# One unit of exponentials per segment on GpSimd: a transformer block on one core

## The chip, the cores and the metric

The kernel runs on one core of a Trainium2 chip. Its engines are TensorE (PE in the profile, with its weight loads as PEld), VectorE (DVE), ScalarE (ACT), GpSimd (POOL) and SyncE (SP), which issues the DMAs. The metric is the device time of one execution in microseconds. A measurement of this kernel is told apart from no change at 2%.

## What is computed

A pre-norm block on 2048 tokens of width 640: an attention of 32 heads of width 20, then a GLU of inner width 1728 without an activation function. Inputs are bf16, of small random values.

```python
def _A_ref(x, wqkv, wo):                       # H = 32, Dh = 20
    q, k, v = split_heads(x @ wqkv)
    p = softmax(einsum("bhqd,bhkd->bhqk", q, k) * Dh ** -0.5)
    return merge_heads(einsum("bhqk,bhkd->bhqd", p, v)) @ wo

def _B_ref(x, w_gate, w_up, w_down):
    return ((x @ w_gate) * (x @ w_up)) @ w_down

h  = x + _A_ref(_layernorm(x), wqkv, wo)
h2 = h + _B_ref(_layernorm(h), w_gate, w_up, w_down)
```

The softmax needs 32 x 2048 x 2048 exponentials, 134 million. That is the work that the change touches.

## The kernel before

**Units, tiles, segments.** The queries are cut into 4 blocks of 512 (`b`), the heads into 8 groups of 4 (`g`), the keys into 16 tiles of 128 (`kt`). A *unit* is the score block of one head, one key tile and one query block: 128 keys on the partitions by 512 queries. All 2048 units stand in one list, in the order b, g, kt, head in the group (`j`). A *segment* is one (b, g), so 64 units; there are 32. The list is cut into *tiles* of three units, without regard to where segments begin, which makes 683 tiles.

**One round of the loop.** For each tile, `emit_S` allocates a score tile `sc` of three PSUM banks (there are two such tiles), lets PE compute three score blocks (L285, K = 32 rows each, in separate row groups of the array), and lets ACT take the exponential of all 1536 columns at once, into a bf16 tile `E` in SBUF (L292; six buffers). There is no maximum subtracted; the scale is in the activation. The three units then wait in the queue `av_q`. Next, `go_on` lets a job that has begun run on for up to 640 ns of estimated PE work. `emit_AV` takes at most four units of tiles at least two rounds old and multiplies each with V, and a column of ones for the sums, into the accumulator `acc` (L330, one PSUM bank, the four heads on separate column groups). At a segment's end DVE copies `acc` to `asb` (L337), and `norm` sends the sums through DRAM and back, so that they lie on all partitions; five rounds later DVE takes their reciprocal (L305), and eight rounds after that it multiplies (L313) `asb` by the spread reciprocals into `On`.

**Jobs.** Everything else on PE comes as jobs in between: the transposes and projections of the first part, and for each finished query block the output projection with the residual and the second layer norm (`job_out`), the GLU (`job_glu`) and the down projection (`job_y`). They share one PSUM bank `mi`, which DVE empties (L167, L464, L509, L525), so a next job's matmuls wait until DVE has done that. The last query block's jobs run after the loop, on the banks of `sc`, and ACT empties the GLU's first product there (`u`, L507).

**Order.** The program's order is the order of emission: each engine runs its own instructions in that order and waits on semaphores for other engines. S of tile i+2 needs the PSUM of tile i, so it waits for tile i's exponential. GpSimd only fills constants before the loop: the identity and the ones of V (L113 to L115).

Of the kernel before, what the change touches and what calls it, by code (L numbers as in the profile page):

```python
# [9 lines left out]
BF16 = mybir.dt.bfloat16  # L10
F32 = mybir.dt.float32
I32 = mybir.dt.int32
ACT = mybir.ActivationFunctionType
ALU = mybir.AluOpType

P = 128
# [4 lines left out]
NT = S // P  # L21
# [7 lines left out]
QB = 512  # L29
NB = S // QB  # L30
TPB = QB // P
UPT = 3
# [3 lines left out]
SM_SCALE = float(DH) ** -0.5  # L36
# [8 lines left out]
def kernel(  # L45
# [11 lines left out]
    nc = tc.nc  # L57
# [5 lines left out]
    pool = lambda name, bufs=1, **kw: ctx.enter_context(tc.tile_pool(name=name, bufs=bufs, **kw))  # L63
    dram = pool("dram", 2, space=bass.MemoryType.DRAM)
    const = pool("const")
# [3 lines left out]
    ep = pool("ep", 6)  # L69
    nrm = pool("nrm", 2)  # L70
    small = pool("small", 2)
    scp = pool("scp", 2, space=bass.MemoryType.PSUM)
    accp = pool("accp", 1, space=bass.MemoryType.PSUM)
    mip = pool("mip", 1, space=bass.MemoryType.PSUM)
# [3 lines left out]
    rx = tc.alloc_tile_pool(name="rx", bufs=2, side="right")  # L78

    ident = const.tile([P, P], BF16, name="ident")  # L80
    make_identity(nc, ident[:])
    wo = [const.tile([P, D], BF16, name=f"wo{g}") for g in range(NG)]

# [79 lines left out]
    def evac(eng, dst, src):  # L163
        if eng == "act":
            nc.scalar.copy(dst, src)  # L165
        else:
            nc.vector.tensor_copy(dst, src)  # L167
# [3 lines left out]
    def bank(dt=F32, w=512):  # L171
        if not end["on"]:
            return mip.tile([P, w], dt, name="mi", tag="mi")

        if end["k"] == UPT:
            end["t"], end["k"] = scp.tile([P, UPT * 512], F32, name="sc"), 0
        k = end["k"]
        end["k"] += 1
        ps = end["t"][:, k * 512:(k + 1) * 512]
        return ps if dt == F32 else ps.bitcast(dt)[:, 0:w]  # L180
# [33 lines left out]
    units = [(b, g, kt, j) for b in range(NB) for g in range(NG) for kt in range(NT) for j in range(HPG)]  # L214
    tiles = [units[i:i + UPT] for i in range(0, len(units), UPT)]
    av_q = deque()
    acc = {"key": None, "t": None, "from": 0}
    done = set()
    jobs = deque()
# [21 lines left out]
    def step():  # L241

        if cur["gen"] is None:
            if not jobs:
                return None
            cur["key"], cur["gen"] = jobs.popleft()
        try:
            c = next(cur["gen"])
        except StopIteration:
            done.add(cur["key"])  # L250
            cur["gen"], c = None, END
        cur["fresh"] = c in (END, NEXT)
        return c

    def ensure(key):
        while key not in done:
            if step() is None:
                raise RuntimeError(f"no job for {key}")
# [20 lines left out]
    def emit_S(i):  # L279
        sc = scp.tile([P, UPT * 512], F32, name="sc")  # L280
        for b, g, kt, j in tiles[i]:
            ensure(("k", g, kt // TPB))
            ensure(("q", b, g))
        for k, (b, g, kt, j) in enumerate(tiles[i]):
            nc.tensor.matmul(  # L285
                sc[:, k * 512:k * 512 + QB],
                lhsT=kT[g][SLOT * j:SLOT * (j + 1), kt * P:(kt + 1) * P],
                rhs=qT[g][SLOT * j:SLOT * (j + 1), b * QB:(b + 1) * QB],
                start=True, stop=True)
        n = len(tiles[i]) * 512  # L290
        e = ep.tile([P, UPT * 512], BF16, name="E")
        nc.scalar.activation(e[:, 0:n], sc[:, 0:n], ACT.Exp, scale=SM_SCALE)  # L292
        for k, u in enumerate(tiles[i]):
            av_q.append((i, u, e[:, k * 512:k * 512 + QB]))

    def norm(b, g, asb):

        r16 = nrm.tile([P, 16], F32, name="r16")
        sums = dram.tile([HPG, QB], F32, name="sums")
        nc.sync.dma_start(sums[:], asb[DH:P:SLOT, :])  # L300
        nc.sync.dma_start(r16[:], sums[:].rearrange("j (c f) -> (j c) f", f=16))

        def back():
            ri = nrm.tile([P, 16], F32, name="ri")
            nc.vector.reciprocal(ri[:], r16[:])  # L305
            scr = dram.tile([HPG, QB], F32, name="scr")
            nc.sync.dma_start(scr[:].rearrange("j (c f) -> (j c) f", f=16), ri[:])
            bc = nrm.tile([P, QB], F32, name="bc")
            for j in range(HPG):
                nc.sync.dma_start(bc[SLOT * j:SLOT * (j + 1), :], scr[j:j + 1, :].to_broadcast([SLOT, QB]))  # L310

            def mult():
                nc.vector.tensor_tensor(On[b % 2][g][:], asb[:], bc[:], ALU.mult)  # L313
                done.add(("n", b, g))
            later(8, mult)
        later(5, back)

    def emit_AV(upto, most):
        n = 0
        while av_q and av_q[0][0] <= upto and n < most:  # L320
            i, (b, g, kt, j), e = av_q[0]
            if acc["key"] != (b, g):
                if now["i"] < acc["from"]:
                    break
                acc["key"] = (b, g)
                acc["t"] = accp.tile([P, QB], F32, name="acc")
            ensure(("v", kt, g // (NG // 2)))
            av_q.popleft()
            h = HPG * g + j
            nc.tensor.matmul(  # L330
                acc["t"][SLOT * j:SLOT * (j + 1), :],
                lhsT=vx[kt][:, VS * h:VS * h + SLOT], rhs=e,
                start=(kt == 0), stop=(kt == NT - 1))
            n += 1
            if kt == NT - 1 and j == HPG - 1:
                asb = nrm.tile([P, QB], F32, name="asb")
                nc.vector.tensor_copy(asb[:], acc["t"][:])  # L337
                norm(b, g, asb)
                acc["key"] = None
                acc["from"] = now["i"] + 2  # L340
                break
        return n
# [139 lines left out]
    def load_w(fp, st):  # L482
        w = min(FPW, FF - fp * FPW)
        st["w", fp] = []
        for nm, src in (("wu", B_w_up), ("wg", B_w_gate)):
            wt = late["w"].tile([P, KT, FPW], BF16, name=nm)
            nc.sync.dma_start(wt[:, :, 0:w], src[:, fp * FPW:fp * FPW + w].rearrange("(c p) f -> p c f", p=P))
            st["w", fp].append(wt)

    def job_glu(b, st):  # L490
        hp, sp = late["h"], late["s"]
        st["hh"] = [hp.tile([P, QB], BF16, name=f"hh{f}") for f in range(2 * FP)]
        for fp in range(FP):
            w = min(FPW, FF - fp * FPW)
            if fp + 1 < FP:
                load_w(fp + 1, st)
            for f2 in range(2):
                M = min(P, w - f2 * P)
                for k in range(2):
                    ps = bank()  # L500
                    for c in range(KT):
                        nc.tensor.matmul(ps[0:M, :], lhsT=st["w", fp][k][:, c, f2 * P:f2 * P + M], rhs=st["ln2T"][:, c, :],  # L502
                                         start=(c == 0), stop=(c == KT - 1))
                        if c == KT - 1:
                            if k == 0:
                                u = sp.tile([P, QB], F32, name="u")
                                evac("act" if end["on"] else "dve", u[0:M, :], ps[0:M, :])  # L507
                            else:
                                nc.vector.tensor_tensor(st["hh"][2 * fp + f2][0:M, :], ps[0:M, :], u[0:M, :], ALU.mult)  # L509
                        yield 216  # L510
                    yield NEXT
# [19 lines left out]
    def add_tail(b):  # L531
        st = {}
        if b == 0:
            do(("open",), open_late)
        do(("load", b), lambda: (load_tail(b, st), load_w(0, st)))
        add(("out", b), job_out(b, st))
        add(("glu", b), job_glu(b, st))
        add(("y", b), job_y(b, st))
# [5 lines left out]
    i = 0  # L544
    while i < n_tiles or av_q:
        now["i"] = i
        if i < n_tiles:
            emit_S(i)
        used = go_on(BUDGET)
        emit_AV(i - 2, 4)  # L550
        run_events(i)
        if b_seen < NB and ("n", b_seen, NG - 1) in done:
            add_tail(b_seen)
            b_seen += 1
        if not used:
            begin(START)
        i += 1
# [39 lines left out]
```

## Time and profile before

| what | value |
|---|---|
| device time, two runs | 1119.3 and 1120.42 us, median 1119.86 |
| span of the profiled execution | 1124.7 us (no other time of it is given) |
| mean granted TensorE clock in it | 0.814 of full speed |
| L285 scores on PE | 2048 matmuls, mean 460 ns, 323.3 us |
| L330 multiplication with V on PE | 2048 matmuls, mean 470 ns, 311.3 us |
| L337 copy of `acc` on DVE | 32, mean 688 ns |
| L313 normalising product on DVE | 32, mean 685 ns |
| L509 GLU product on DVE | 42, mean 691 ns |

The records of PE overlap: matmuls of different row or column groups run beside each other, and their ends are modelled, so counts times means exceed the busy time. The records of ACT overlap too, since one exponential starts before the former is written out. A wait is put down to the engine that released it. In a slice line each digit is a fortieth of the span, in tenths; the clock line is what the throttle granted to TensorE.

### The profile page before, as it was taken

To read this page: it belongs to the slowest core of one execution; us is meant where nothing else is said; L and a number is where in the kernel's file an instruction comes from. 1 tells how busy PE (TensorE), PEld (TensorE's weight loads), DVE (VectorE), ACT (ScalarE), POOL (GpSimd) and SP (SyncE) were. 2 spreads that over 40 slices of the span, in tenths; PEclk is the share of its full clock that TensorE was granted. 3 is DMA by queue.
4 is the path that set the end of the run, shared out by engine and by line. 5 is a ranking of instruction groups with operands and counts; after the bars stand their busy time and mean duration, and the time that the engine had idled before them with its cause. 6 is when DMAs were issued, how large, how long until landed. Compare 5 with 4: busy or idle time off the path is not lost.

```text
span 1124.7 us, 14910 instructions
## 1 busy us (share of the span) xinstructions
PE 978.5 (87%) x6000; PEld 322.7 (29%) x6000; DVE 296.2 (26%) x690; ACT 953.1 (85%) x726; POOL 3.4 (0%) x54
## 2 busy tenths in 40 slices
PE   3768999999889999978899999888999998884667
PEld 1222332222223223322232234222332233222224
DVE  6452333322005332100034321100253321003211
ACT  4456999999999999999999999999999999990010
POOL 1000000000000000000000000000000000000000
PEclk9668999999558999955588999755779998556699
DMA  4000000100041220100111210000112200003120
GB/s 158 24 1 1 11 11 11 31 20 11 11 136 35 57 71 16 35 11 11 58 34 33 60 51 24 22 11 26 33 34 63 71 17 28 11 11 81 45 66 24
DMA packets 63493, 41.19 MB, mean 37 GB/s; under 512 B 18688, under 2 KB 58560, under 8 KB 63424
## 3 DMA queue, kind: packets, MB, share of 16 engines
q1 hardware_dynamic: 63424, 40.24, 12.7%
q8 instruction: 47, 0.77, 0.3%
q14 instruction: 22, 0.18, 0.1%
HBM read 37.08 MB, written 3.15 MB: 36 GB/s over the span
## 4 chain that ended last, share of the span: by engine, by line
PE 48%; ACT 36%; issue 8%; DVE 5%; DMA 1%; SPq 1%; DVEq 0%; ACTq 0%
ACT E L292 35%; PE sc L285 10%; PE acc L330 9%; PE mi L502 6%; PE mi L195 5%; PE mi L522 5%; PE sc L502 3%; PE mi L461 3%; PE sc L522 2%; PE mi L205 1%; PE mi L185 1%; DVE st L121 1%; ACT lnT L165 1%; PE sc L461 1%; DVE hh L509 1%
## 5 line engine op out<-in xcount | busy, mean ns | idle before, releaser
L292 ACT ACTIVATE E<-sc 128x1536 bf16<-128x1536 f32 (+1 forms) x683 | 925.5, 1692 | 47.5 <-PE sc L285 45.8
L285 PE MATMUL sc<-qT,kT 32*128 32x512 bf16 x2048 | 323.3, 460 | 63.7 <-ACT E L292 59.1
L330 PE MATMUL acc<-E,vx 128*32 128x512 bf16 x2048 | 311.3, 470 | 0.5 <-ACT E L292 0.5
L285 PEld LDWEIGHTS <-kT 32*128 32x128 bf16 x2048 | 99.3, 94 | 297.8 <-issue 293.0
L330 PEld LDWEIGHTS <-vx 128*32 128x32 bf16 x2048 | 67.3, 96 | 224.5 <-issue 221.2
L195 PE MATMUL mi<-lnT,wp 128*128 128x512 bf16 x310 | 91.6, 398 | 5.3 <-DVE qT L167 2.7
L165 ACT COPY u<-sc 128x512 f32<-128x512 f32 (+1 forms) x14 | 8.2, 585 | 80.9 <-PE sc L502 80.9
L337 DVE COPY asb<-acc 128x512 f32<-128x512 f32 x32 | 22.0, 688 | 167.7 <-PE acc L330 167.6
L502 PE MATMUL mi<-ln2T,wu 128*128 128x512 bf16 (+1 forms) x210 | 62.0, 394 | 0.4
L522 PE MATMUL mi<-wd,hh 128*128 128x320 bf16 x336 | 60.6, 302 | 0.0
L502 PE MATMUL mi<-ln2T,wg 128*128 128x512 bf16 (+1 forms) x210 | 60.0, 383 | 0.1
L167 DVE COPY u<-mi 128x512 f32<-128x512 f32 (+1 forms) x42 | 29.0, 691 | 79.1 <-PE mi L502 79.1
L509 DVE TENSOR_TENSOR hh<-mi,u 128x512 bf16<-128x512 f32 (+1 forms) x42 | 29.0, 691 | 77.1 <-PE mi L502 77.1
L522 PEld LDWEIGHTS <-hh 128*128 128x128 bf16 x448 | 37.5, 97 | 39.6 <-issue 28.8
L205 PE MATMUL mi<-wv,lnT 128*128 128x320 bf16 x160 | 34.8, 360 | 8.8 <-DVE vx L167 8.7
L167 DVE CAST kT<-mi 128x512 bf16<-128x512 f32 x31 | 21.4, 691 | 65.7 <-PE mi L195 65.7
L461 PE MATMUL mi<-wo,on 128*128 128x320 bf16 x192 | 37.6, 323 | 0.0
L195 PEld LDWEIGHTS <-wp 128*128 128x128 bf16 x320 | 23.2, 100 | 46.4 <-issue 38.7
L313 DVE TENSOR_TENSOR on<-asb,bc 128x512 bf16<-128x512 f32 x32 | 21.9, 685 | 55.2 <-DMA bc<-scr 55.2
L167 DVE CAST qT<-mi 128x512 bf16<-128x512 f32 x31 | 21.3, 687 | 53.7 <-PE mi L195 53.7
L502 PEld LDWEIGHTS <-wu 128*128 128x128 bf16 (+1 forms) x280 | 21.7, 101 | 45.8 <-issue 35.2
L502 PEld LDWEIGHTS <-wg 128*128 128x128 bf16 (+1 forms) x280 | 21.4, 100 | 42.4 <-issue 31.8
(58 smaller groups left out, 338.8 us busy)
## 6 DMA issues: line engine op xcount, KB each, us to landing
bc<-scr SPq DMA_DIRECT2D x128, 64.0 KB
wu<-in_B_w_up_dram SPq DMA_DIRECT2D x24, 320.0 KB
wg<-in_B_w_gate_dram SPq DMA_DIRECT2D x24, 320.0 KB
xs<-in_A_x_dram SPq DMA_DIRECT2D x4, 640.0 KB
xr<-in_A_x_dram SPq DMA_DIRECT2D x16, 160.0 KB
out_dram<-xr SPq DMA_DIRECT2D x16, 160.0 KB
wd<-in_B_w_down_dram SPq DMA_DIRECT2D x13, 160.0 KB
E<-in_A_wqkv_dram SPq DMA_DIRECT2D x5, 320.0 KB
```

Source lines behind the costliest of these rows:

```text
L167: nc.vector.tensor_copy(dst, src)
L195: nc.tensor.matmul(ps[:], lhsT=wpad[m][c][:].rearrange("p h e -> p (h e)")[:, g * P:(g + 1) * P], rhs=lnT[:, c, ch * QB:(ch + 1) * QB], st ...
L205: nc.tensor.matmul(ps[:, 0:HALF], lhsT=lnT[:, c, t * P:(t + 1) * P], rhs=wv[c][:, half * HALF:(half + 1) * HALF], start=(c == 0), stop=(c ...
L285: nc.tensor.matmul(sc[:, k * 512:k * 512 + QB], lhsT=kT[g][SLOT * j:SLOT * (j + 1), kt * P:(kt + 1) * P], rhs=qT[g][SLOT * j:SLOT * (j + 1 ...
L292: nc.scalar.activation(e[:, 0:n], sc[:, 0:n], ACT.Exp, scale=SM_SCALE)
L313: nc.vector.tensor_tensor(On[b % 2][g][:], asb[:], bc[:], ALU.mult)
L330: nc.tensor.matmul(acc["t"][SLOT * j:SLOT * (j + 1), :], lhsT=vx[kt][:, VS * h:VS * h + SLOT], rhs=e, start=(kt == 0), stop=(kt == NT - 1))
L337: nc.vector.tensor_copy(asb[:], acc["t"][:])
L461: nc.tensor.matmul(ps[:, 0:HALF], lhsT=On[b % 2][g][:, t * P:(t + 1) * P], rhs=wo[g][:, cs], start=(g == 0), stop=(g == NG - 1))
L502: nc.tensor.matmul(ps[0:M, :], lhsT=st["w", fp][k][:, c, f2 * P:f2 * P + M], rhs=st["ln2T"][:, c, :], start=(c == 0), stop=(c == KT - 1))
L509: nc.vector.tensor_tensor(st["hh"][2 * fp + f2][0:M, :], ps[0:M, :], u[0:M, :], ALU.mult)
L522: nc.tensor.matmul(ps[:, 0:HALF], lhsT=st["hh"][f][0:K, t * P:(t + 1) * P], rhs=late["Wd"][f][0:K, cs], start=(f == 0), stop=(f == 2 * FP ...
```

## The change

In tiles that hold three units of key tile 1 of a segment, the third unit's columns are left out of ACT's exponential. DVE copies them from PSUM to SBUF as fp32, scaled (`xp`); GpSimd raises e to them, elementwise, into a bf16 tile `apart`. Because tiles do not begin with segments, such a tile exists in the segments whose number leaves 1 or 2 when divided by 3, which are 21 of 32. The unit is held back from `av_q` and put in front of it when the first unit of the segment's last key tile comes up. Both new tiles have one buffer. The GLU's `u` becomes bf16 with one buffer, where it had fp32 and two.

```diff
+    powp = pool("powp", 1)
...
+    base_e = const.tile([P, 1], F32, name="base_e")
+    nc.gpsimd.memset(base_e[:], 2.718281828459045)
...
+    held = {}
...
         n = len(tiles[i]) * 512
         e = ep.tile([P, UPT * 512], BF16, name="E")
+        apart = None
+        if len(tiles[i]) == UPT and tiles[i][2][2] == 1 and tiles[i][0][2] == 1:
+            n -= 512
+            xp = powp.tile([P, 512], F32, name="xp")
+            nc.vector.tensor_scalar(xp[:], sc[:, n:n + 512], SM_SCALE, None, ALU.mult)
+            apart = powp.tile([P, 512], BF16, name="apart")
+            nc.gpsimd.tensor_tensor(apart[:], base_e[:].to_broadcast([P, 512]), xp[:], ALU.pow)
         nc.scalar.activation(e[:, 0:n], sc[:, 0:n], ACT.Exp, scale=SM_SCALE)
         for k, u in enumerate(tiles[i]):
-            av_q.append((i, u, e[:, k * 512:k * 512 + QB]))
+            if apart is not None and k == 2:
+                held[u[0:2]] = (i, u, apart[:])
+            else:
+                av_q.append((i, u, e[:, k * 512:k * 512 + QB]))
...
                 acc["t"] = accp.tile([P, QB], F32, name="acc")
+            if kt == NT - 1 and (b, g) in held:
+                av_q.appendleft(held.pop((b, g)))
+                continue
             ensure(("v", kt, g // (NG // 2)))
...
                             if k == 0:
-                                u = sp.tile([P, QB], F32, name="u")
+                                u = sp.tile([P, QB], BF16, name="u", bufs=1)
                                 evac("act" if end["on"] else "dve", u[0:M, :], ps[0:M, :])
```

## The prediction

> **What bounds the kernel now.** I read the busy shares and the slices of the page first, then the list of waits, then the exponential's row and its timeline, and last the timeline around the tiles that the change touches.
>
> ```profile
> PE 978.5 (87%) x6000; PEld 322.7 (29%) x6000; DVE 296.2 (26%) x690; ACT 953.1 (85%) x726; POOL 3.4 (0%) x54
> ...
> ACT  4456999999999999999999999999999999990010
> POOL 1000000000000000000000000000000000000000
> PEclk9668999999558999955588999755779998556699
> ```
>
> ACT is full from slice 5 to 36, some 110 to 1010 us. POOL does nothing after the first slice. TensorE's granted clock is one half in four stretches.
>
> ```profile
> L292 ACT ACTIVATE E<-sc 128x1536 bf16<-128x1536 f32 (+1 forms) x683 | 925.5, 1692 | 47.5 <-PE sc L285 45.8
> ...
> PE sc L285 <- ACT E L292: 59.1, 235, 0.9
> ACT E L292 <- PE sc L285: 45.8, 39, 5.3
> ```
>
> In the list of waits, PE waits for the exponential (a score tile to come free) 235 times; ACT waits for scores only 39 times. So in the middle the exponentials set the pace, and PE sets it only in places. What one exponential is worth comes from the timeline of ACT, and from the one row that has a 1024-column form, the last of the loop:
>
> ```profile
> 398.48 16.48 ACT L292 ACTIVATE E<-sc 128x1536 bf16<-128x1536 f32 x12
> ...
> 601.26 1.45 ACT L292 ACTIVATE E<-sc 128x1536 bf16<-128x1536 f32 x1 [0.28 <-PE sc L285]
> ...
> L292 ACT ACTIVATE E<-sc x6: 1490/1917/1921, 1002.3 to 1009.0; 128x1536 bf16<-128x1536 f32 x5, 128x1024 bf16<-128x1024 f32 x1
> ```
>
> Twelve in a row take 16.48 us, so one follows another every (16.48 - 1.69)/11 = 1.34 us (1.69 is the mean record, which overlaps the one before). One that starts on an idle ACT takes 1.45. In the third line, for the loop's last six, the single 1024-column record is 1.49 against 1.92 beside it: 512 columns less are 0.43 us less. So a shortened one takes 0.92 in a full queue and 1.02 from idle.
>
> **The change, part by part.** *Removed:* 21 times 0.43 = 9.0 us of ACT, if ACT sets the end at each of the 21 tiles and nothing comes in front. *Added in front:* in the changed program the shortened exponential no longer waits for PE but for DVE, with the count that DVE's new copy of the third bank raises. The copy and the exponential read different banks, but they run one after the other. So the path score, exponential becomes score, copy, exponential. No row shows this copy; the nearest are the 512-column DVE operations from PSUM, 0.688 to 0.691 us (L337, L167, L509), and I take 0.69. DVE starts 0.04 us after the matmul's end in such rows (asb at 399.65 below, after an L330 group that ends at 399.61). From DVE's end to ACT's start I take 0.05, as from ACT's end to PE's start. Three kinds of tile follow; S is the score group of L285:
>
> ```profile
> 398.89 0.39 PE L285 MATMUL sc<-qT,kT 32*128 32x512 bf16 x3
> ...
> 399.65 0.69 DVE L337 COPY asb<-acc 128x512 f32<-128x512 f32 x1 [0.38 <-PE acc L330]
> ...
> 368.91 5.75 ACT L292 ACTIVATE E<-sc 128x1536 bf16<-128x1536 f32 x4 [1.03 <-PE sc L285]
> ...
> 371.37 0.39 PE L285 MATMUL sc<-qT,kT 32*128 32x512 bf16 x3
> ...
> 485.88 0.61 PE L285 MATMUL sc<-qT,kT 32*128 32x512 bf16 x3 [0.18 <-ACT E L292]
> ```
>
> Full clock, PE waiting for ACT (six tiles, near 194, 282, 400, 633, 661, 897 us). S starts 0.05 after the exponential two before ended (398.84) and ends at 399.28. Copy 399.32 to 400.01, exponential from 400.06, which would be done from idle at 401.08. The exponential before it ends at 398.84 + 1.34 = 400.18, so the queue gives 401.10. The copy is hidden, and 0.43 is gained: 6 x 0.43 = 2.6.
>
> Half clock (six, near 310, 487, 545, 721, 749, 984). S runs 0.61, to 486.49; copy to 487.22; exponential 487.27 to 488.29, where before it ended at 485.83 + 2 x 1.34 = 488.51. Gain 0.22: 6 x 0.22 = 1.3.
>
> PE late (nine, near 106, 135, 222, 372, 458, 575, 808, 839, 925). At 372 the exponential two before ended at 368.91 + 1.45 = 370.36, but S starts at 371.37, one us late, and ends at 371.76. Before, the exponential began 0.11 later and took 1.45, to 373.32; now it begins at 372.54 and ends at 373.56. That loses 0.25. The nine by the same steps give from +0.12 (222) to -0.48 (135, DVE busy with another copy), together -1.8.
>
> Sum: 2.6 + 1.3 - 1.8 = 2.1 us gained. If the copy were always hidden it is 9.0; if it never were, a loss of 21 x 0.25 = 5.3.
>
> *The pow.* 21 instructions on an engine that is otherwise empty. Nothing of its kind is in the trace; the nearest rows are
>
> ```profile
> masks.py:199 POOL TENSOR_SCALAR_AFFINE_SELECT ident<-ident 128x128 bf16<-128x128 bf16 x1 | 0.3, 292 | 0.1
> ...
> L114 POOL MEMSET vx<- 128x11 bf16 x16 | 2.7, 287 | 0.0
> ```
>
> By the first (2.3 ns an element) 512 elements are 1.2 us; by the second, with all of it put on its 11 elements (26 ns), 13.4 us. Its reader is the multiplication at the segment's end, in the changed order behind the score group 20 tiles later: by the times of those L285 groups 24.7 to 28.8 us after the copy, 26.5 on average. The next copy into the same buffer comes 26.7 us later at the earliest. Both ends of the price lie below that room, so I cost the pow at nothing. The work that hides it is twenty tiles of exponentials; with that cover gone, each us beyond costs a us per segment. But neither row is a power: the upper end is no bound that I trust, and this is the largest unknown here.
>
> The Trainium skill (GPSIMD Engine Reference, Performance versus the Vector engine) gives about 2.6 cycles an element for two inputs at 1.2 GHz and calls GpSimd the wrong engine for elementwise work; that estimate is 1.1 us and would leave the sum as it is, but the page prices an add and no power.
>
> *Moved:* 21 multiplications (L330), from their place to the end of their segment; PE's count stays 6000, and the cover is PE's waiting for ACT. Where PE is late, one of a group of four (0.40 us) is 0.1 us: at most 21 x 0.1 = 2. *Queues:* the copy stands in DVE's queue ahead of an asb copy or an evacuation; these come 0.69 later, against idle time before L509 of 77.1/42 = 1.8 us. Its wait for the former pow would hold those and the exponential. *The GLU's u* in bf16 with one buffer: in the loop DVE writes and reads it in order; in the tail ACT's copy (585 ns, 14 times) now waits for the product (0.69) of the group before, while PE runs five matmuls (over 1 us). Nothing; with no cover, 14 x 0.69 = 9.7.
>
> The profiled span is 1124.7 us, 4.9 above the median 1119.86 of the unprofiled runs; I take the gain off the median: 1119.9 - 2.1 = 1118.
>
> **Rivals.** *One: the copy costs nothing,* and the whole 9.0 us come: 1111. For it, DVE is 26% busy; against it, the exponential's new wait and the nine late tiles.
>
> *Two: the pow outlasts its room.* PE then stops at the multiplication of `apart`, in order, with all score groups behind it; ACT runs dry some 1.3 us later, and DVE's next copy waits too. It decides from 2% = 22.4 us, or 1.07 us in each of 21 segments: a pow of 27.5 us, 54 ns an element, twice the upper row. At 30 us it is 21 x 3.5 = 74, 1192; at 40 us 21 x 13.5 = 284, 1402. For it: a power is many steps in software, and no row excludes it. Against: the rows.
>
> *Three: a long pow holds DVE up,* though within its room. No row has both engines at work after the first slice. The normalising product on DVE (L313) reads two SBUF tiles and comes late in the pow's time; in the segment whose copy would end at 135.6 us it comes 17.8 us later, and an evacuation that PE waits for 2 us behind it:
>
> ```profile
> 153.44 0.68 DVE L313 TENSOR_TENSOR on<-asb,bc 128x512 bf16<-128x512 f32 x1
> 155.43 0.69 DVE L167 CAST kT<-mi 128x512 bf16<-128x512 f32 x1 [1.30 <-PE mi L195]
> ```
>
> If that product has to wait until the pow ends, a pow of 22 us holds it 22 - 17.8 = 4.2 us; less the 2 us, in the 15 segments that are not at half clock (there PE has no such jobs), that is 33 us: 1152. Below 18 us of pow it is nothing; against it, one such product in a segment is all that could be held in most of them.
>
> The Trainium skill (SBUF — State Buffer, Who interferes with whom) has a rule that speaks against this change: a DVE instruction with two SBUF inputs is blocked entirely while a GpSimd instruction that reads SBUF runs. By it the sum is this rival's wherever the pow is longer than 18 us; without it the sum stays.
>
> **How the numbers follow.** Forecast (1118, its own range 1111 to 1124) 0.50; rival one 0.10; rival two 0.30; rival three 0.10, most of it over 2%. What a measurement of this kernel can tell from no change is taken as 2%, 22 us. Faster by that is out of reach (9.0 at most): 0.01. Slower: 0.30 + 0.08 = 0.38. Within: 0.61. The range begins at 1110; above, it must take in half of the slow cases, to a pow of about 31 us, 21 x 4.5 = 94: 1213.
>
> **What would show it.** POOL's row for `apart`: its mean below 18 us keeps rivals two and three out, above 27 us makes two certain; then PE's list of waits has `acc` waiting for `apart`, ACT's busy slices fall below 9, and PEclk drops more often. The forecast shows in 22 exponentials of 1024 columns, in ACT's waits for `xp` at the nine late tiles alone, and in an unchanged L285 wait. I am wrong in the copy's part if ACT waits for `xp` at nearly all 21, or none.

## The result, and the profile after

The changed kernel takes 2291.58 us (median of 2 runs, 2291.51 to 2291.65) against 1119.86 us: a ratio of 2.044, 95% interval 2.038 to 2.051. The span of the profiled execution is 2289.9 us. The first lines of its page, busy shares and slices:

```profile
PE 1001.3 (44%) x5947; PEld 319.6 (14%) x6000; DVE 309.7 (14%) x711; ACT 948.4 (41%) x726; POOL 1723.7 (75%) x76
...
ACT  5535181373427136342722724272272437228101
POOL 0199769949976994997799499679949967994900
PEclk8767595675568568655565867655565768555579
```

PE and ACT are busy for about as long as before, 1001 and 948 us, in twice the span. (PE's count is 5947 and not 6000 because 53 records are missing from the profile; the 6000 weight loads are all there.) What is new is POOL, at 75%. ACT's slices are no longer nines: it works in bursts and stands still between them. The row of POOL among the costliest groups:

```profile
L302 POOL TENSOR_TENSOR apart<-base_e,xp 128x512 bf16<-128x512 f32 x21 | 1720.3, 81917 | 456.4 <-DVE xp L300 456.4
```

And of the list of waits (us in total, times, longest) the long ones of PE and ACT:

```profile
PE acc L347 <- POOL apart L302: 1147.0, 21, 56.1
...
ACT E L303 <- PE sc L289: 599.0, 64, 56.2
ACT E L303 <- DVE xp L300: 566.2, 17, 57.5
```

One power takes 81.9 us, and PE stops in front of each of the 21 multiplications of `apart`, 54.6 us on average. ACT's two waits add up to 1165 us, but they are PE's wait handed on: scores don't come, or the next segment's copy of them doesn't. The timeline of the first such segment shows the whole mechanism:

```profile
105.09 81.93 POOL L302 TENSOR_TENSOR apart<-base_e,xp 128x512 bf16<-128x512 f32 x1 [101.07 <-DVE xp L300]
...
122.58 0.68 DVE L327 TENSOR_TENSOR on<-asb,bc 128x512 bf16<-128x512 f32 x1
...
122.94 0.85 PE L208 MATMUL mi<-wv,lnT 128*128 128x320 bf16 x5
...
187.07 0.58 PE L347 MATMUL acc<-apart,vx 128*32 128x512 bf16 x1 [55.16 <-POOL apart L302]
...
187.62 1.51 PE L208 MATMUL mi<-wv,lnT 128*128 128x320 bf16 x5
...
190.58 1.02 ACT L303 ACTIVATE E<-sc 128x1024 bf16<-128x1024 f32 x1 [57.43 <-DVE xp L300]
```

POOL starts at 105.09. PE reaches the multiplication after 26.8 us and then waits 55.16. When it goes on, its five L208 matmuls take 1.51 us, where they took 0.85 before the stop: TensorE has also lost its clock. The granted clock is 1.00 for the first 3 us of this stop, 0.50 from 140 us to its end and on to 193 us, and 1.00 again from 195. PE goes on at 0.50 after all 21 stops; over the whole profile, stops included, the mean is 0.659, where it was 0.814.

### The profile page after: what moved, and what is told of

Its sections match the earlier page's. It is cut to its first block, busy times and chain, and to the rows that moved or that the text cites. A ratio compares the mean times of both kernels' runs of the same rounds, so it can differ in the third digit from the quotient of the medians.

```text
span 2289.9 us, 14949 instructions
## 1 busy us (share of the span) xinstructions
PE 1001.3 (44%) x5947; PEld 319.6 (14%) x6000; DVE 309.7 (14%) x711; ACT 948.4 (41%) x726; POOL 1723.7 (75%) x76
## 4 chain that ended last, share of the span: by engine, by line
POOL 72%; PE 15%; POOLq 4%; ACT 3%; DVE 3%; issue 3%; DMA 0%; SPq 0%; DVEq 0%; ACTq 0%
POOL apart L302 72%; POOLq L609 4%; PE sc L289 3%; PE acc L347 3%; ACT E L303 2%; PE mi L519 2%; PE mi L198 2%; PE sc L519 2%; PE mi L539 1%; PE sc L539 1%; PE mi L478 1%; PE mi L208 1%; DVE xp L300 1%; DVE st L124 0%; ACT lnT L168 0%
## 5 line engine op out<-in xcount | busy, mean ns | idle before, releaser
L302 POOL TENSOR_TENSOR apart<-base_e,xp 128x512 bf16<-128x512 f32 x21 | 1720.3, 81917 | 456.4 <-DVE xp L300 456.4
L347 PE MATMUL acc<-apart,vx 128*32 128x512 bf16 x21 | 12.3, 584 | 1147.0 <-POOL apart L302 1147.0
L347 PE MATMUL acc<-E,vx 128*32 128x512 bf16 x2027 | 331.2, 475 | 0.2 <-ACT E L303 0.2
L289 PEld LDWEIGHTS <-kT 32*128 32x128 bf16 x2048 | 92.0, 94 | 303.2 <-issue 298.7
L300 DVE TENSOR_SCALAR xp<-sc 128x512 f32<-128x512 f32 x21 | 14.5, 692 | 606.5 <-PE sc L289 606.0
L168 ACT CAST u<-sc 128x512 bf16<-128x512 f32 (+1 forms) x14 | 8.2, 585 | 132.0 <-PE sc L519 132.0
L170 DVE CAST u<-mi 128x512 bf16<-128x512 f32 (+1 forms) x42 | 29.0, 691 | 134.2 <-PE mi L519 134.2
L208 PE MATMUL mi<-wv,lnT 128*128 128x320 bf16 x160 | 35.5, 366 | 8.7 <-DVE vx L170 8.6
```

Source lines behind the costliest of these rows:

```text
L208: nc.tensor.matmul(ps[:, 0:HALF], lhsT=lnT[:, c, t * P:(t + 1) * P], rhs=wv[c][:, half * HALF:(half + 1) * HALF], start=(c == 0), stop=(c ...
L289: nc.tensor.matmul(sc[:, k * 512:k * 512 + QB], lhsT=kT[g][SLOT * j:SLOT * (j + 1), kt * P:(kt + 1) * P], rhs=qT[g][SLOT * j:SLOT * (j + 1 ...
L300: nc.vector.tensor_scalar(xp[:], sc[:, n:n + 512], SM_SCALE, None, ALU.mult)
L302: nc.gpsimd.tensor_tensor(apart[:], base_e[:].to_broadcast([P, 512]), xp[:], ALU.pow)
L347: nc.tensor.matmul(acc["t"][SLOT * j:SLOT * (j + 1), :], lhsT=vx[kt][:, VS * h:VS * h + SLOT], rhs=e, start=(kt == 0), stop=(kt == NT - 1))
```

## The experiments

Twelve kernels, in four groups that each ran on one chip with the kernel before beside them. A ratio is to that kernel's median, with its 95% interval in brackets. Only the runs with 256 columns, with the early reader and the last one differ from the kernel before by more than 2%. The others are read by their intervals, and differences of a few microseconds between them with care: single executions of one kernel lie up to 11 us apart (run 7, 1112.91 to 1123.84).

**1. The same change with a multiplication in the power's place.**

```diff
-            nc.gpsimd.tensor_tensor(apart[:], base_e[:].to_broadcast([P, 512]), xp[:], ALU.pow)
+            nc.gpsimd.tensor_tensor(apart[:], base_e[:].to_broadcast([P, 512]), xp[:], ALU.mult)
```

> The changed kernel with a multiplication in the place of the power on GpSimd: same copy, same operands, same waits; one unit in 21 segments isn't exponentiated. Theory (the power's length beyond its room of 26.5 us is the whole loss): GpSimd's instruction takes 1 to 2 us, PE never waits for apart, and what is left is the forecast's own sum, 1117.8 us (2.1 less than before). Rival (the rest of the change costs too: the exponential behind the copy, the moved multiplication, the narrower u): above 1122 us.

Measured 1119.41 us, ratio 0.9995 (0.9984 to 1.0005). GpSimd's instruction, as the list of the tile's instructions gives it (count, shortest/median/longest in ns, first and last start):

```profile
L302 POOL TENSOR_TENSOR apart<-base_e,xp x21: 1040/1041/1042, 103.4 to 981.6; 128x512 bf16<-128x512 f32 x21
```

And ACT's wait for the copy, in the list of waits:

```profile
ACT E L303 <- DVE xp L300: 8.8, 16, 1.1
```

With the power gone, so is the loss. Everything else in the change together is worth between 1.8 us less and 0.6 us more than before; 2.1 less was forecast, just outside. The operands, the broadcast base and the bf16 result are the same here, so the 81.9 us are the power's own.

**2 and 3. The power of fewer columns.** The filling is done by GpSimd ahead of the copy's result.

```diff
+            nc.gpsimd.memset(apart[:, 128:512], 1.0)
-            nc.gpsimd.tensor_tensor(apart[:], base_e[:].to_broadcast([P, 512]), xp[:], ALU.pow)
+            nc.gpsimd.tensor_tensor(apart[:, 0:128], base_e[:].to_broadcast([P, 128]), xp[:, 0:128], ALU.pow)
```

(and the same with 256.) With 128 columns:

> The power of the first 128 of the 512 columns alone; the other 384 are filled with ones, so their exponentials are left out. Theory (160 ns a column, room 26.5 us): a power of 20.5 us, inside the room, so no wait of PE for apart and 1118 us, as with the multiplication. Rival (a running power holds DVE's normalising product, which comes 17.8 us after the copy): that product starts up to 2.7 us later in its segment and the time is some 10 us above that of the multiplication. Rival (the cost is per instruction and not per column): about 80 us each and 2290 us.

With 256 columns:

> The power of the first 256 columns alone, the other 256 filled with ones. Theory: 41.0 us a power, and with 0.3 us for the filling 41.3 - 26.5 = 14.8 us of waiting in each of 21 segments, 311 us: 1429 us. Rival (cost per instruction): 2290 us. Rival (GpSimd only ever delays by its DVE neighbours): well under 1300 us.

Measured 1118.83 us with 128 columns, ratio 0.998 (0.9965 to 0.9995), and 1436.62 with 256, ratio 1.282 (1.279 to 1.285). From the list of the tile's instructions of the first:

```profile
L303 POOL TENSOR_TENSOR apart<-base_e,xp x21: 20717/20717/20732, 103.8 to 978.0; 128x128 bf16<-128x128 f32 x21
```

And of the second:

```profile
L303 POOL TENSOR_TENSOR apart<-base_e,xp x21: 41115/41115/41131, 104.5 to 1283.9; 128x256 bf16<-128x256 f32 x21
```

The second's list of waits has PE at the multiplication of `apart`:

```profile
PE acc L348 <- POOL apart L303: 289.8, 21, 15.3
```

20.72, 41.12 and 81.92 us for 128, 256 and 512 columns lie on one line: 61.2/384 = 159 ns a column and 0.3 us. POOL at 40% of the span costs nothing as long as each power ends inside its room; at 61% it costs 317 us. So neither GpSimd's load nor a disturbance of its neighbours is the loss, but what sticks out of the room. With 128 columns PE has no wait for `apart` at all, and the third rival's hold of DVE doesn't appear in the time.

**4. The same 20.7 us power, its reader moved forward.**

```diff
-            if kt == NT - 1 and (b, g) in held:
+            if kt == NT // 2 and (b, g) in held:
```

> As the power of 128 columns (20.7 us each, inside its room, 1118.8 us; the other 384 columns are ones), but multiplied when the segment's ninth key tile comes up and not at its last. By the times of the score groups before, the reader then stands 13.2 to 16.6 us after the copy, 14.0 on average. Theory (the loss is the power's length less its room): 140 us in all, 1259 us, with 21 waits of PE for apart of 6.7 us each. Rival (what counts is only how long GpSimd runs): 1119 us, as before.

Measured 1278.04 us, ratio 1.141 (1.138 to 1.144). The wait in the list of waits:

```profile
PE acc L348 <- POOL apart L303: 136.8, 21, 7.2
```

GpSimd does exactly what it did in the 128-column run, and the kernel is 159 us slower, because the reader comes 12 us sooner. The waits sum to 136.8 us, as expected from 140; the time rose by 22 us more than that. The same is left over in the other kernels that stop. Against run 1, the 256 columns cost 27 us and the whole power 25 us more than PE's waits for `apart`. So a stop costs 1.1 to 1.3 us besides its length, whether it lasts 6.5, 14 or 55 us. PE goes on at half clock after all 21 stops of each of the three, for 2.8 us or more; this is a likely cause, but no run separates it.

**5 and 6. The shortened exponential alone.** No copy and no GpSimd instruction; the unit's weights are a constant tile of ones.

```diff
+    ones = const.tile([P, 512], BF16, name="ones")
+    nc.gpsimd.memset(ones[:], 1.0)
...
-            xp = powp.tile([P, 512], F32, name="xp")
-            nc.vector.tensor_scalar(xp[:], sc[:, n:n + 512], SM_SCALE, None, ALU.mult)
-            apart = powp.tile([P, 512], BF16, name="apart")
-            nc.gpsimd.tensor_tensor(apart[:], base_e[:].to_broadcast([P, 512]), xp[:], ALU.pow)
+            apart = ones
```

> The shortened exponential alone: no copy and no GpSimd instruction, the unit's weights are a constant tile of ones, multiplied at the segment's end as in the changed kernel; 21 units' exponentials are left out. Theory (0.43 us of ACT per shortened exponential, nothing in front of it): up to 9.0 us less than before, 1111 us, and 7 us less than with the multiplication, which is what the copy in front costs. Rival (PE sets the end there, and ACT's saving is lost): 1117 us or more, no difference from the multiplication.

And with the unit multiplied where it stood before the change:

```diff
-                held[u[0:2]] = (i, u, apart[:])
+                av_q.append((i, u, apart[:]))
```

> As the kernel without copy and power (constant weights for the unit, 1115.9 us), but multiplied in its place and not at the segment's end; 21 units' exponentials are left out. Theory (the moved multiplication is free, and half of the 9 us is lost where PE is late): the same within 1.5 us, 1114 to 1117 us. Rival (the moved multiplication ate it): 1111 us.

Measured 1115.90 us held to the segment's end, ratio 0.996 (0.9943 to 0.9977), and 1110.67 in place, ratio 0.9916 (0.9893 to 0.9939), which is 9.3 us less than the kernel before (6.8 to 12.0 by the interval). The first lies between its theory and its rival. The second theory, no difference, fell: held, the median is 5.2 us higher, though PE does the same number of matmuls.

The two profiles don't show this as a cost of the held multiplication. Counted from the first exponential, the loop's last one ends 4.9 us earlier in place. Of these, 2.2 are there by the end of tile 20, and the first changed tile is 23. Another 2.3 arise at tiles 116 and 117: TensorE's granted clock from 233.5 to 236.5 us is 0.50 in the held kernel's profile, as it is there in the kernel before, and 1.00 in the other. From tile 120 on the two stay level. (The held kernel's profile is of the slowest of its executions, 1120.67 us.)

The changed tiles can be read by themselves, against the same tiles before: from the end of the exponential two ahead of the changed one to the end of the third behind it. In place, 0.43 us is gained at each of the twelve tiles where PE isn't late, and 0.8 at the nine late ones together, 5.9 in all. Held, it is 5.4.

**7. The approximate exponential on DVE, 21 tiles.** One instruction makes the unit's weights from PSUM, into `E` itself; no `xp`, no `apart`, nothing held. It works because the bits of a bf16 number, read as an integer, rise nearly in step with its logarithm: a score that is scaled, shifted and rounded to an integer has nearly the bits of its exponential.

```diff
+EXP_A = 128.0 * 1.4426950408889634
+EXP_B = 127.0 * 128.0 - 7.3
...
+        if len(tiles[i]) == UPT and tiles[i][2][2] == 1 and tiles[i][0][2] == 1:
+            n -= 512
+            nc.vector.tensor_scalar(e[:, n:n + 512].bitcast(I16), sc[:, n:n + 512], SM_SCALE * EXP_A, EXP_B, ALU.mult, ALU.add)
         nc.scalar.activation(e[:, 0:n], sc[:, 0:n], ACT.Exp, scale=SM_SCALE)
```

> No GpSimd: in the same 21 tiles DVE itself makes the third unit's weights from PSUM in one instruction (scale and offset, rounded to int16, the bits read as bf16; an approximate exponential, 1.8% spread), into the exponential's own tile; nothing is held back. Theory: DVE's 0.69 us stand in front of the exponential as the copy did, so it is as with the multiplication on GpSimd, 1116 to 1120 us. Rival (the moved multiplication and not the copy in front ate the saving): 1111 to 1115 us.

Measured 1119.64 us, ratio 0.999 (0.9973 to 1.0007). Nothing is moved here, and yet 0.65 us is left of the 9.3. Read at the changed tiles as above, 1.6 us is left of the 5.9: 2.2 gained at the six tiles at full clock, 1.0 gained at the six at half clock, 1.6 lost at the nine late ones. So a DVE instruction in front of the exponential eats most of the saving by itself.

**8. The copy behind the exponential.** As the first run, with the activation issued before the copy.

> As the multiplication in the power's place (1119.4 us), but ACT's exponential is issued before DVE's copy, so the copy waits for the exponential and not the other way round. Theory (the copy in front of the exponential costs what the nine late tiles lost): the exponential starts as early as before; the score tile comes free when the copy ends, 0.37 us later than before, which PE doesn't have at full clock with jobs. So no better: 1118 to 1122 us. Rival (the order alone was the cost): 1115 us, as without the copy.

Measured 1130.20 us, ratio 1.009 (1.008 to 1.010), worse than either expectation. The timeline of one such tile:

```profile
401.40 0.69 DVE L302 TENSOR_SCALAR xp<-sc 128x512 f32<-128x512 f32 x1 [1.94 <-ACT E L299]
402.01 0.68 DVE L355 COPY asb<-acc 128x512 f32<-128x512 f32 x1
402.15 0.39 PE L289 MATMUL sc<-qT,kT 32*128 32x512 bf16 x3 [0.61 <-DVE xp L302]
```

Now PE waits for the copy before it can reuse the banks (12 times, 10.9 us in all), and what stands behind the copy on DVE waits too.

**9. The narrower u.**

```diff
-                                u = sp.tile([P, QB], F32, name="u")
+                                u = sp.tile([P, QB], BF16, name="u", bufs=1)
```

> The kernel before with the one edit on the GLU's u: bf16 and one buffer. Theory: nothing, 1120 us within 2 us. Rival (ACT's copy waits for the product of the group before in the part after the loop): up to 9.7 us more.

Measured 1119.39 us, ratio 0.9987 (0.997 to 1.0005): nothing.

**10 to 12. The approximate exponential on DVE in more tiles.** The edit of run 7, in every second full tile (341 units), in every third (228), and in every second but issued behind ACT's exponential.

> The same approximate exponential on DVE in every second full tile (341 units). Theory: ACT's work falls by 341 x 0.43 = 147 us, but PE sets the pace next: it waited 59 us for ACT in the whole run and at half clock its own rounds take 1.34 us. So 20 to 60 us less, 1060 to 1100 us. Rival (the wait of the exponential behind DVE, 0.25 us where PE is late, and evacuations that queue behind DVE's work, eat it): 1120 us or more.

> The approximate exponential on DVE, issued before ACT's, in every third tile (228 units instead of 341). Theory (in the half-taken version PE already sets the pace, 1.30 us a tile at full clock against 1.34 of ACT alone): most of the 15 us is there already, 1103 to 1110 us. Rival (ACT still sets the pace and the gain goes with the count): two thirds of it, 1110 us or more.

> As the approximate exponential on DVE in 341 tiles (1104.9 us), but issued after ACT's exponential of the same tile. Theory (each tile's PSUM is then held for 0.92 + 0.8 us instead of 0.7 + 1.0, about the same, but ACT no longer starts late): within 10 us of it, 1095 to 1110 us. Rival (score tiles come free too late): 1120 us or more.

Measured 1104.87 us with 341 units, ratio 0.9871 (0.9842 to 0.9900); 1110.70 with 228, ratio 0.9933 (0.9917 to 0.9950); 1232.50 with 341 behind ACT, ratio 1.101 (1.100 to 1.103). The first is the fastest kernel of the study, with approximate weights for a sixth of the units. Its line of busy times:

```profile
PE 967.0 (87%) x6000; PEld 314.8 (28%) x6000; DVE 515.0 (46%) x1031; ACT 836.6 (75%) x726; POOL 3.4 (0%) x54
```

And ACT's waits in the loop, from the list of waits:

```profile
ACT E L298 <- DVE E L297: 137.2, 321, 7.5
...
ACT E L298 <- PE sc L288: 12.8, 13, 3.8
```

ACT's work fell by 953.1 - 836.6 = 117 us, and its waits in the loop rose from 45.8 us to 137.2 + 12.8 = 150, nearly all for DVE; that leaves 12 us, where the medians differ by 15 and 20 to 60 were expected. From 228 to 341 units the gain went from 8 to 15 us, with the count; so it isn't used up at 228, as I had expected. The expectation also read PE's rounds at half clock as 1.34 us long: in the kernel before, 0.18 of each is a wait for ACT, and with 341 units a round takes 1.26 there (490 to 560 us). Issued behind ACT it is not near the first but 10% slower than before: DVE's instruction now waits for ACT in nearly every one of these tiles, and PE waits for DVE, for the score tile and for the emptying of `mi`, which stands behind that instruction:

```profile
DVE E L299 <- ACT E L297: 577.7, 332, 3.8
...
PE sc L288 <- DVE E L299: 35.0, 110, 0.9
PE mi L198 <- DVE qT L170: 28.8, 30, 1.3
PE mi L509 <- DVE u L170: 26.8, 30, 1.3
```

## Why the prediction was wrong

**The step that failed is the price of the power: "so I cost the pow at nothing".** It rested on two rows of POOL that are no powers, with 1.2 and 13.4 us as ends, both under the room. Measured are 81.9 us, six times the upper end and three times the room. The room itself was right: 26.5 us on average in the text, 26.8 in the timeline above, 27.4 on average in that profile. The text called this the largest unknown and gave the case beyond the room 0.30, with 27.5 us as its threshold; but the likeliest case and the range followed the two rows, and the range was cut at a power of about 31 us.

**The second rival was right, by its own formula.** 1118 + 21 x (81.9 - 26.5) = 2281 us, where 2291.58 was measured. The same formula gave 1429 for 256 columns (1436.62) and 1259 for the early reader (1278.04). It is short by 8 to 19 us each time: it has no term for what a stop costs besides its length. The half clock after each stop is seen, its share isn't settled.

**The shortened exponential** is worth the 0.43 us that was worked out, at each of the twelve tiles where PE isn't late. At the nine late ones nearly all of it is lost even with nothing in front. So the 9.3 us of run 6 agree with the 9.0 in part by luck: 5.9 lie at the changed tiles, and where the rest comes from stays open.

**The copy in front of the exponential** was sized about right: it was to leave 2.1 of the 9.0 us, and with a DVE instruction in front and nothing moved 0.65 is left by the medians, from 3.0 us gained to 0.8 us lost by the interval. Kind by kind, run 7's profile has 2.2, 1.0 and -1.6 us where the sum had 2.6, 1.3 and -1.8. ACT waits for `xp` 16 times in run 1 and not only at the nine late tiles. That follows from the prediction's own sum at half clock, in which the exponential starts 0.10 us after the one before has ended; with these six tiles there are fifteen such waits.

**The moved multiplication** was costed at nothing, at most 2 us; beside the copy it cost about that. The changed tiles of run 1, which has both, lose 0.9 us where those of run 7 gain 1.6. Of this difference of 2.5 us, 1.7 lie at ten tiles, those that follow a segment with a held unit: there that unit's multiplication comes 0.8 to 1.7 us ahead of the next copy, and so ahead of the scores that the copy and the exponential wait for. At the other tiles it lies 30 us or so back. The 5.2 us between the medians of runs 5 and 6, without the copy, aren't seen at the changed tiles (5.4 against 5.9), and their cause stays open.

**The narrower u** at nothing: right.

**DVE held up by a running power** (the third rival): no. The normalising product, which reads two SBUF tiles, starts at 122.58 in the timeline above, in the middle of a power that runs from 105.09 to 187.02, and takes 0.68 us. 21 of the 32 such products run inside a power, and over all 32 the shortest, median and longest are

```profile
L327 DVE TENSOR_TENSOR on<-asb,bc x32: 681/682/694, 122.6 to 2190.9; 128x512 bf16<-128x512 f32 x32
```

against 679/682/693 before. The rule of the Trainium skill (SBUF — State Buffer, Who interferes with whom), that such an instruction is blocked entirely while a GpSimd instruction that reads SBUF runs, doesn't hold for this power; here the measurement decides. The skill's figure for a two-input elementwise operation (GPSIMD Engine Reference, Performance versus the Vector engine) does agree: 1.1 us by the estimate from it for 512 columns, 1.04 measured for the multiplication. The error was to lean on neighbours in kind of instruction, not in kind of arithmetic. (The third rival's sum has a slip: 33 us above 1118 are 1151, not 1152.)

## What to carry to other kernels

An operation without a row has no price, and a neighbour's row is no bound on it: measure it alone, on one tile, before work is built around it, and write down beside it the time until its first reader comes. An engine that is idle helps only if each piece of work ends before that reader. Its load alone doesn't tell: a 20.7 us piece cost nothing or 159 us depending on where its reader stood. Where a helper takes part of a tile from a saturated engine, look which of the two then waits for the other: a short wait in front of the saturated engine can eat most of the saving, and the helper queued behind the saturated engine can cost far more than it saves.

## What the runs showed of the hardware

GpSimd's elementwise power costs 159 ns a column of 128 partitions, 0.3 us besides (20.72, 41.12 and 81.92 us for 128, 256 and 512 columns), the same to within 0.02 us at each length; its multiplication of the same operands costs 1.04 us for 512 columns, 79 times less.

A power that runs for 82 us doesn't slow DVE's instructions beside it: the 21 products of two SBUF tiles that lie inside one take 681 to 694 ns, and 679 to 693 before.

TensorE's granted clock fell with PE's stops. Its mean over the profile, stops included, is 0.659 with 21 stops of 55 us, 0.751 with stops of 14, 0.783 with stops of 6.5 and 0.825 without, with 128 columns. In the stop shown above it fell to one half 3.7 us after PE stopped, and it stayed there for 6.5 us after PE went on.
